# Turning five of the seven blocks of an FFT stage by DMA transposes: a long-convolution layer's backward pass on one Trainium2 core

## The chip, the cores and the metric

The program runs on one core of a Trainium2 chip. The metric is device time in microseconds (us), the median of several runs. One further execution was recorded by the hardware profiler; times inside the kernel are counted from the start of that execution's span.

## What is computed

The reference runs a small network forward and returns its output and the gradients of eight inputs. Two layers A (a gated long convolution) and B (a dense block) alternate, each around a layer norm and a residual; both A layers share their weights, and so do both B layers.

```python
def A(q, k, v, shift_k, ssm_k, ssm_D):        # B=1, S=2048, D=448
    k_shift = sum(shifted(k, t) * shift_k[:, 3 - t] for t in range(4))
    kv = k_shift * v
    y = irfft(rfft(pad(kv)) * rfft(pad(ssm_k)))[:S]   # FFT of length 4096
    return q * (y + kv * ssm_D)

def B(x, w1, w2):                             # F=1792
    return silu(x @ w1) @ w2

x = A_q
x = x + A(layernorm(x), ...);  x = x + B(layernorm(x), w1, w2)
x = x + A(layernorm(x), ...);  x = x + B(layernorm(x), w1, w2)
# outputs: x, and d(x . grad_out) / d(A_q, A_k, A_v, shift_k, ssm_k, ssm_D, w1, w2)
```

All tensors are bf16. The convolution's own gradient needs the spectrum of the output gradient, its products with the saved spectra of `kv` and of `ssm_k`, and two inverse transforms.

## The kernel before

The work is in three parts.

**Prefix** (`_ssm_prefix`): the spectra of `ssm_k` and `kv`, the convolution's output, and stores of the spectra to DRAM. Here two blocks of an FFT stage are already turned by DMA transposes (L426), the other five on TensorE.

**Main** (`Main.run`): forward and backward of the layers over four chunks of 512 rows. The dense layers' operands for the weight gradients are turned by DMA transposes on SP's queue (`store`, L595: one of 128x2048 elements, 512 KB, and one of 128x1536, 384 KB, per half) and written to DRAM (`put`, L601).

**Suffix** (`_ssm_suffix`): the convolution's backward pass. The output gradient's FFT has two stages. The first (`_s1_gy`, L218) is a set of matmuls whose results are copied into `A1g`, a tile of 128 partitions by 14336 elements, seen as 7 blocks of 16 squares of 128x128. Every square must be turned before the second stage. In the loop `for g in range(7)` at L1177, `_turn64` (L225) does that on TensorE: 32 transposes of half a row block each into PSUM, and one copy of 128x2048 (`_copy`, L116 on ACT or L117 on DVE, chosen by a running balance `bal`) into the block `Z[g]` of the tile `B1v`. Then `spectrum(cp)` runs the second stage for block `cp` (L236) and writes it back over `Z[cp]` (L1191), and `inverse(cp, ...)` multiplies by the saved spectra and runs the first inverse stage (L265). Its results go to `B1k`, which lies over the memory of `A1g`, and to `B1v`. So `A1g` may be overwritten only once all blocks have been turned out of it.

**Jobs.** TensorE's order is the program's (`manual_schedule`). Wherever the suffix would leave TensorE waiting it calls `jobs.run(n)`, which issues n groups of four matmuls of the weight gradients (`mms`, L1038, tile `ps_d`). Every output tile of a weight gradient takes two sets of 16 such matmuls; each set reads one stationary tile `dstat` of 128x2048 elements, 512 KB, that `load` (L1030) brings from DRAM on SP's queue. There are four slots for `dstat`, used in turn, so a load waits until the set that read its slot four loads earlier has been issued and done:

```python
st = self.stat[:, self.n_st % 4]
self.last_ld = nc.sync.dma_start(out=st, in_=src[:, ft, :, :])
```

SP's queue is worked off in the order of the program: an instruction that waits there holds back all that follow. At the change, the order on this queue in the program of before is: four `dstat` loads, the last at 516.56 us, then the load at 521.32, the load at 527.07, the load at 531.44, the load of `n3m` (L1099, 1792 KB), and further `dstat` loads. The saved spectra (`spec_load`, L1172 and L1173) come on POOL's queue.

Of the kernel before, what the change touches and what calls it, by code (L numbers as in the profile page):

```python
# [11 lines left out]
BF16 = mybir.dt.bfloat16  # L12
# [5 lines left out]
P = 128  # L18
# [95 lines left out]
def _copy(nc, eng, out, in_):  # L114
    if eng is nc.scalar:
        return nc.scalar.copy(out, in_)  # L116
    return eng.tensor_copy(out, in_)  # L117
# [18 lines left out]
def kernel(  # L136
# [63 lines left out]
    with tc.manual_schedule(engines={nc.tensor.engine}):  # L200
        with ExitStack() as es:
            Main(k, es).run(ys)
        _ssm_suffix(k)
# [18 lines left out]
def _turn64(k, pt, i, src):  # L222
    for r in range(2):
        rs = slice(64 * r, 64 * r + 64)
        k.nc.tensor.transpose(pt[:, r, i, :], src[rs], k.ident[rs, rs])  # L225
# [912 lines left out]
def _ssm_suffix(k):  # L1138
    nc, tc, bal = k.nc, k.tc, k.bal
# [3 lines left out]
    psum = k.psum  # L1143
    mm = dict(tag="mm", bufs=2)
    k.pt = dict(s1=mm, s2=mm, v=mm)
    A1 = k.A1g
    with ExitStack() as es:
# [12 lines left out]
        Z = [B1v_[:, 16 * g:16 * g + 16, :] for g in range(7)]  # L1160
# [3 lines left out]
        A1f = A1[:].rearrange("p a c n s -> p (a c n s)").rearrange("p (a b) -> p a b", b=P)  # L1164

        def spec_load(cp):
            lo, hi = cp * 2048, (cp + 1) * 2048
            if cp % 2:
                kk = [kk1[:, i] for i in range(2)]
            else:  # L1170
                kk = [sp.tile([P, 2048], BF16, name="kk_d", tag="gK", bufs=2)[:] for i in range(2)]
            nc.gpsimd.dma_start(out=kk[0], in_=k.SPEC_d["K"][:, lo:hi])  # L1172
            k.last_sp = nc.gpsimd.dma_start(out=kk[1], in_=k.SPEC_d["KV"][:, lo:hi])  # L1173
            return kk

        kks = [spec_load(0)]
        for g in range(7):  # L1177
            pt = psum.tile([P, 2, 16, 64], BF16, name="ps_tr", **mm)
            for i in range(16):
                _turn64(k, pt, i, A1f[:, 16 * g + i, :])  # L1180
            _copy(nc, bal.pick(2048, dve_ns=0.53), Z[g].rearrange("p i (r x) -> p r i x", r=2), pt[:])
            jobs.run(1)
        kks.append(spec_load(1))

# [182 lines left out]
```

## Time and profile before

| | |
|---|---|
| Median of 3 runs | 704.69 us (704.58 to 705.24) |
| The profiled execution's own time | 704.52 us |
| Its span, first to last instruction | 702.7 us |
| Granted TensorE clock, mean | 0.997 |
| PE (matmul) busy | 671.8 us, 96% |
| PE weight loads busy | 359.8 us, 51% |
| DVE / ACT / POOL busy | 484.3 / 432.2 / 101.0 us |
| Hardware DMA queue q1 (SP and ACT) | 111.78 MB, 58.3% of 16 engines' span |
| Software DMA queue q0 (POOL) | 36.29 MB, 15.2% |
| Instruction fetches, queue q8 | 46 packets, 0.75 MB |

The profiled execution takes 1.82 us more than its span, and 0.17 us less than the median of the runs. A busy PE says little by itself, since matmuls overlap; the chain of waits and the timeline of a stage say what the stage waits for. A DMA's row gives the time in which its queue's engine issued it, and apart from that the time from issue to landing. Losses on SP's queue do not show as idle time of SP.

### The profile page before, as it was taken

Reading aid. Unit: us, or ns where it says so; the run is one execution under the profiler, and the core shown is the slowest. Engines: PE = TensorE matmul, PEld = TensorE weight load, DVE = VectorE, ACT = ScalarE, POOL = GpSimd, SP = SyncE. Lnnn points to the kernel's source line nnn. Section 1 sums busy time; section 2 is a strip of 40 time slices with the busy share of each in tenths; the row PEclk is TensorE's granted clock in tenths of the full one; section 3 lists DMA queues with packets and bytes.
Section 4 is the critical chain, followed back from the end, with each engine's and each line's share of the span. In section 5 each row is a group of like instructions: output and inputs, shape, how many; then the busy total and the mean of one; then the engine's idle time right before and its main releaser. Section 6 shows DMA issues by size and latency. Waiting matters only on the chain.

```text
span 702.7 us, 14555 instructions
## 1 busy us (share of the span) xinstructions
PE 671.8 (96%) x5897; PEld 359.8 (51%) x5933; DVE 484.3 (69%) x1131; ACT 432.2 (62%) x522; POOL 101.0 (14%) x173
## 2 busy tenths in 40 slices
PE   6998789999999999999999999999999999999996
PEld 5876555454444444444444334444555555555664
DVE  5689862676889948889568884753946555538991
ACT  4988766968866957669577585223655453554431
POOL 1047110110011100111100100010111211102311
PEclk9999999999999999999999999999999999999999
DMA  8999948459898987487676599959567888966981
GB/s 315 260 272 304 351 137 212 112 109 260 217 225 240 245 195 184 137 236 202 203 180 180 159 227 335 288 168 218 187 225 268 309 273 317 349 190 215 330 292 42
DMA packets 199797, 161.03 MB, mean 229 GB/s; under 512 B 147697, under 2 KB 180212, under 8 KB 198962
## 3 DMA queue, kind: packets, MB, share of 16 engines
q1 hardware_dynamic: 184550, 111.78, 58.3%
q0 software_dynamic: 10368, 36.29, 15.2%
q10 hardware_dynamic: 4812, 12.04, 5.2%
q8 instruction: 46, 0.75, 0.4%
q14 instruction: 21, 0.17, 0.1%
HBM read 66.05 MB, written 54.60 MB: 172 GB/s over the span
## 4 chain that ended last, share of the span: by engine, by line
PE 59%; DVE 19%; issue 10%; ACT 5%; DMA 3%; POOL 3%; ACTq 0%; POOLq 0%; DVEq 0%
PE ps_d L1038 18%; PE ps_n L828 9%; PE ps_h L638 7%; PE ps_g L638 6%; PE ps_o L790 5%; DMA w2sb<-in_B_w_dram 3%; DVE ln_st L301 2%; PE ps_v L265 2%; PE ps_cv L449 2%; POOL rstd L306 2%; DVE lb_v L986 2%; PE ps_h L642 2%; DVE n L309 1%; DVE X L794 1%; PE ps_g L642 1%
## 5 line engine op out<-in xcount | busy, mean ns | idle before, releaser
L1038 PEld LDWEIGHTS <-dstat 128*128 128x128 bf16 x896 | 84.0, 98 | 77.8 <-issue 4.0
L828 PE MATMUL ps_n<-w1T,ghT 128*128 128x448 bf16 x448 | 97.0, 353 | 1.6 <-DVE ghT L813 1.3
L790 PE MATMUL ps_o<-w2sb,aT 128*128 128x448 bf16 x448 | 89.3, 353 | 0.2
L638 PE MATMUL ps_h<-nT,w1sb 128*128 128x512 bf16 (+1 forms) x408 | 84.2, 336 | 3.5 <-ACT Dall L116 2.2
L116 ACT CAST ghT<-ps_g 128x1024 bf16<-128x1024 f32 (+1 forms) x54 | 47.8, 900 | 59.4 <-PE ps_g L642 40.2
L638 PE MATMUL ps_g<-nT,w2T 128*128 128x512 bf16 x319 | 78.0, 380 | 2.1 <-DVE Dall L117 0.5
L828 PEld LDWEIGHTS <-ghT 128*128 128x128 bf16 x448 | 40.7, 98 | 50.5 <-issue 8.0
L790 PEld LDWEIGHTS <-aT 128*128 128x128 bf16 x448 | 43.0, 98 | 40.7 <-issue 2.6
L638 PEld LDWEIGHTS <-w1sb 128*128 128x128 bf16 x420 | 39.2, 98 | 39.0 <-issue 9.8
L773 ACT ACTIVATE aT<-ps_h 128x1024 bf16<-128x1024 f32 (+1 forms) x48 | 44.2, 920 | 20.4 <-PE ps_h L642 12.7
L986 DVE SCALAR_TENSOR_TENSOR lb_v<-lb_u,n 128x448 bf16<-128x448 bf16 x60 | 37.2, 619 | 25.4 <-ACT lb_u L832 24.9
L116 ACT CAST Dall<-ps_h 128x1024 bf16<-128x1024 f32 (+2 forms) x60 | 54.3, 906 | 0.0
L783 ACT ACTIVATE Dall<-Dall 128x1024 bf16<-128x1024 bf16 (+1 forms) x48 | 53.2, 1186 | 0.1
L638 PEld LDWEIGHTS <-w2T 128*128 128x128 bf16 x336 | 31.3, 98 | 41.9 <-issue 7.1
L306 POOL TENSOR_TENSOR rstd<-ln_ve,mhalf 128x2 f32<-128x2 f32 (+1 forms) x24 | 19.6, 818 | 220.7 <-DVE ln_ve L305 220.7
L1038 PE MATMUL ps_d<-X,dstat 128*128 128x448 bf16 x224 | 47.9, 353 | 0.0
L1038 PE MATMUL ps_d<-go,dstat 128*128 128x448 bf16 x224 | 47.2, 353 | 0.0
L1038 PE MATMUL ps_d<-n3m,dstat 128*128 128x448 bf16 x224 | 46.4, 353 | 0.0
L1038 PE MATMUL ps_d<-n1m,dstat 128*128 128x448 bf16 x224 | 46.3, 353 | 0.0
L832 ACT ACTIVATE lb_u<-ps_n,rstd 128x448 bf16<-128x448 f32 x32 | 20.6, 644 | 29.1 <-PE ps_n L828 21.2
L116 ACT CAST A1g<-ps_v 128x1024 bf16<-128x1024 f32 x14 | 14.9, 1065 | 36.5 <-PE ps_v L265 36.5
L794 DVE TENSOR_TENSOR X<-X,ps_o 128x448 bf16<-128x448 bf16 x32 | 19.5, 611 | 21.7 <-PE ps_o L790 21.7
(206 smaller groups left out, 1120.2 us busy)
## 6 DMA issues: line engine op xcount, KB each, us to landing
dstat<-a_d SPq DMA_DIRECT2D x28, 512.0 KB, 4.9
dstat<-g_d SPq DMA_DIRECT2D x28, 512.0 KB, 5.4
a_d<-turned SPq DMA_DIRECT2D x16, 512.0 KB, 3.0
g_d<-turned SPq DMA_DIRECT2D x16, 512.0 KB, 3.0
a_d<-turned SPq DMA_DIRECT2D x16, 384.0 KB, 2.7
g_d<-turned SPq DMA_DIRECT2D x16, 384.0 KB, 3.1
spec_K<-KAB POOLq DMA_DIRECT2D x7, 512.0 KB, 5.7
KAB<-KAB POOLq DMA_DIRECT2D x28, 128.0 KB, 5.0
```

The lines of the kernel that those rows point to most:

```text
L116: return nc.scalar.copy(out, in_)
L306: nc.gpsimd.tensor_tensor(out=r[:, lo:hi], in0=ve[:, lo:hi], in1=k.mhalf[:, lo:hi], op=ALU.pow)
L638: self.nc.tensor.matmul(ps, lhsT=w[:, b, ft * P:(ft + 1) * P], rhs=x[:, b], start=(start and b == 0), stop=(stop and b == bs[2]))
L642: self.nc.tensor.matmul(ps, lhsT=w[sl, b, ft * P:(ft + 1) * P], rhs=x[sl, b], start=start, stop=stop)
L773: self.last_silu = nc.scalar.activation(aT[hh][:, o:o + hi - lo, :], ps[:, lo:hi, :], ACT.Silu)
L783: self.nc.scalar.activation(dT[hh][:, o:o + n, :], dT[hh][:, o:o + n, :], ACT.Derivative_silu)
L790: nc.tensor.matmul(po[:, :D], lhsT=aT[ft // 7][:, ft % 7, tl * P:(tl + 1) * P], rhs=self.w2sb[:, ft, :], start=(ft == 0), stop=(ft == NF - 1))
L794: self.last_o = nc.vector.tensor_tensor(out=X[:, t, :], in0=X[:, t, :], in1=po[:, :D], op=ALU.add)
L828: nc.tensor.matmul(pn[:, :D], lhsT=gh[ft // 7][:, ft % 7, tl * P:(tl + 1) * P], rhs=self.w1T[:, ft, :], start=(ft == 0), stop=(ft == NF - 1))
L832: nc.scalar.activation(u0[:], pn[:, :D], ACT.Identity, scale=k.rstd[2 * L + 1][:, t:t + 1], accum_out=cp[:, tl, 0:1])
L986: nc.vector.scalar_tensor_tensor(out=v[:], in0=u0, scalar=-1.0 / D, in1=n_t, op0=ALU.mult, op1=ALU.mult, accum_out=cp[:, 1:2])
L1038: self.nc.tensor.matmul(ps[:, :D], lhsT=st[:, t, :], rhs=mov[:, t, :], start=(first and t == 0), stop=(last and t == NT - 1))
```

## The change

For blocks 2 to 6 the turn on TensorE with its copy is left out. In its place five DMA transposes of 128x2048 elements are put on SP's queue ahead of the loop, each from a block of `A1g` to the same `Z[g]`. Blocks 0 and 1 are turned as before, and the loop's seven `jobs.run(1)` stay.

```diff
         kks = [spec_load(0)]
+        for g in range(2, 7):
+            nc.sync.dma_start_transpose(out=Z[g], in_=A1f[:, 16 * g:16 * g + 16, :].rearrange("p a b -> p (a b)"))
         for g in range(7):
-            pt = psum.tile([P, 2, 16, 64], BF16, name="ps_tr", **mm)
-            for i in range(16):
-                _turn64(k, pt, i, A1f[:, 16 * g + i, :])
-            _copy(nc, bal.pick(2048, dve_ns=0.53), Z[g].rearrange("p i (r x) -> p r i x", r=2), pt[:])
+            if g < 2:
+                pt = psum.tile([P, 2, 16, 64], BF16, name="ps_tr", **mm)
+                for i in range(16):
+                    _turn64(k, pt, i, A1f[:, 16 * g + i, :])
+                _copy(nc, bal.pick(2048, dve_ns=0.53), Z[g].rearrange("p i (r x) -> p r i x", r=2), pt[:])
             jobs.run(1)
         kks.append(spec_load(1))
```

In the built program the five transposes stand on SP's queue between the `dstat` load that went at 516.56 us in the profile of before and the one that went at 521.32. The first of them waits for the copies into `A1g`. The order of all other instructions on PE, DVE, ACT and POOL is that of before, without the five turns and their copies (three on DVE, two on ACT). The first copy into `B1k` (ACT, L116, `A1g<-ps_v`) waits in addition for all five transposes.

## The prediction

> **What bounds the kernel now.** I read the page's chain that ended last first.
>
> ```profile
> PE 59%; DVE 19%; issue 10%; ACT 5%; DMA 3%; POOL 3%; ACTq 0%; POOLq 0%; DVEq 0%
> ```
>
> PE carries it. In order of time the chain lies on PE without a break from 511 to 632 us (ps_d and ps_v alone), then on DVE, and PE's busy time still fills the span to 690. So what the suffix's first half gains or loses on PE moves the end by as much, unless DVE's stretch from 637 to 685 were pinned by something else; it starts when PE's ps_gkv results arrive (DVE sat idle 7.77 us for the first at 633.34), so it moves along.
>
> Next the timeline of the stage, which shows what a turn costs:
>
> ```profile
> 516.99 0.93 ACT L116 CAST A1g<-ps_s 128x896 bf16<-128x896 f32 x1
> ...
> 518.35 0.52 PEld L225 LDWEIGHTS <-A1g 64*128 64x128 bf16 x32 [0.37 <-ACT A1g L116]
> ...
> 519.78 0.52 PEld L225 LDWEIGHTS <-A1g 64*128 64x128 bf16 x32 [0.37 <-issue]
> ...
> 521.80 0.93 PE L1038 MATMUL ps_d<-X,dstat 128*128 128x448 bf16 x4
> ...
> 534.93 3.19 PE L1038 MATMUL ps_d<-go,dstat 128*128 128x448 bf16 x16
> ...
> 537.96 2.43 PE L1038 MATMUL ps_d<-X,dstat 128*128 128x448 bf16 x12
> ```
>
> A1g is complete at 516.99 + 0.93 = 517.92. Turns start 1.43 us apart, with four ps_d matmuls in each step.
>
> Last, SP's queue, the lines of its loads and transposes one at a time. First the dstat loads at 516.56 (call it load A) and 521.32 (load B), then the transposes of L595 at 450.0, 481.2 and 475.2 with the landing line of each, then L426's two.
>
> ```profile
> 516.56 0.32 SPq L1030 DMA_DIRECT2D dstat<-a_d  x1
> 521.32 0.32 SPq L1030 DMA_DIRECT2D dstat<-a_d  x1
> ...
> L595 SPq DMA_TRANSPOSE turned<-ghT x1: 1610/1610/1610, 450.0 to 450.0; - x1
> DMA to landing us min/median/max: 3.8/3.8/3.8
> ...
> L595 SPq DMA_TRANSPOSE turned<-ghT x1: 1557/1557/1557, 481.2 to 481.2; - x1
> DMA to landing us min/median/max: 3.9/3.9/3.9
> ...
> L595 SPq DMA_TRANSPOSE turned<-ghT x1: 1783/1783/1783, 475.2 to 475.2; - x1
> DMA to landing us min/median/max: 5.4/5.4/5.4
> ...
> L426 SPq DMA_TRANSPOSE KAB<-KAB x2: 3879/4429/4979, 21.7 to 26.8; - x2
> DMA to landing us min/median/max: 7.6/8.0/8.4
> ```
>
> L426's two have the shape and the kind (SBUF to SBUF) of the new five; L595's larger half has it too. Issue takes 1.4 to 6.1 us, landing 3.3 to 8.4.
>
> **The change, part by part.**
>
> *Removed from PE.* Sixteen ps_d matmuls take 537.96 - 534.93 = 3.03 us, so four take 0.76. A turn thus costs 1.43 - 0.76 = 0.67 us, its 0.37 us of idle weight loading included. Five give 3.4 us. The copies (three of 1.22 us on DVE, two of 1.86 on ACT) cost nothing before and bring nothing: both engines then wait for PE (DVE 4.18 us before its next product). All PE work from 521.2 on could come 3.4 us earlier.
>
> *Added to SP.* Five transposes stand between load A and load B. The first can start when A1g is complete, at about 518.0. All dstat loads from B on, and n3m, are queued behind them. B's slot is free at 521.3, so before it left at 521.32; now it leaves when the fifth transpose has been issued, and its data come after theirs.
>
> *Who waits for that.* With four slots, load B is read by the fourth set after the one that ended at 521.3: X from 521.80, go from 527.55, X from 531.25, and go from 534.93. Load B is thus due at 534.93 before, and at 534.93 - 3.4 = 531.5 after. The cover of B is 531.5 - 521.3 = 10.2 us, against a landing of 3.4 to 8.2 us in this stage. Load A is due at 531.25 - 3.4 = 527.8 and lands 6.7 us after 516.56, at 523.3: safe.
>
> *When the transposes are through.* Pace: the two that follow each other from 450.0 move 896 KB, at 282 to 292 GB/s in nearly every slice of that window, in about 3.5 us: 2.0 us per 512 KB. Start: with nothing ahead, the first lands 3.8 us after issue, 521.8. With load A ahead it is later: the transpose at 418.7, behind a dstat load and a store, landed after 7.1 us, and those of L426 stood behind the input loads. Load A shares its engines with POOL's spectra until 521 and lands at 523.3; I take the first transpose to be through one pace later, 525.3. That is 7.3 us after issue, near the 7.1 row. Then four more at 2.0: 533.3.
>
> *Load B.* The dstat load issued at 482.82, right behind the transpose of 481.16, landed 4.0 us later, at 486.8; the transpose itself landed at 481.16 + 3.9 = 485.1. So a load lands 1.7 us after the transpose ahead of it. Load B lands at 533.3 + 1.7 = 535.0 and PE stands still for 535.0 - 531.5 = 3.5 us. The next load follows by one pace of a load (512 KB at the 400 GB/s of this stage's full slices, 1.3 us) and is due 3.03 us later; n3m is used only with the first g_d loads (from 568). No second stall in this sum.
>
> *Sum.* 704.52 - 3.4 + 3.5 = 704.6, which is 704.8 on the scale of the median (0.17 above the profiled run). With a first transpose a little less held back by load A (half a microsecond) it is 704.3. I take 704.6.
>
> *Bounds of the unknown term.* Best: load A does not hold the first transpose; the last lands at 521.8 + 4 x 2.0 = 529.8, B at 531.5, no stall. Worst: the pace of L426, 4.43 us of SP's time each; B leaves at 518.0 + 22.1 = 540.1 and lands 3.4 us later, 543.5: a stall of 12.0.
>
> *Edits that cost nothing.* Z[2] is read first by the second stage at 547.91 before, 544.5 after; even the worst case has it by 530. The copy into B1k that now waits for all five transposes is due at 541.02 - 3.4 = 537.6, 4.3 us after my last landing; beyond that it would hold ACT, but B's stall moves it along. A1g's memory is not touched earlier.
>
> *A rule for the speed of a transpose.* The trace's rate is 282 to 292 GB/s while one runs alone. [...]
>
> **The rivals.**
>
> *Faster, 701.3 to 703.2: the transposes run beside load A.* The queue has 16 engines, and transposes could start on those that are done with A. Stall 0 to 2.0 us, time 704.69 - 3.4 + 0 to 2.0. For it: L595's median landing is 4.1 us, though many of its transposes follow other traffic. Against: the 7.1 to 8.4 us rows above.
>
> *Slower, 706.1 to 709.3: one held-up engine holds up the whole transpose.* The transpose at 475.2 lasted 5.4 us to landing, not 3.8:
>
> ```profile
> GB/s 421 393 418 430 440 461 346 237 144 106 293 288 258 242 398 270 270 266 51 9 0 0 0 2 7 10 9 10 9 65 292 292 287 278 16 0 0 0 0 0
> ...
> q8 instruction: 1, 0.02, 1.5%
> ```
>
> In this window (475 to 481 us, 0.15 us a slice) the rate falls to 0 for 1.5 us in the middle of the transpose, and one instruction fetch lies in it. In 518 to 531 us before there were two such fetches. They are 16 KB, and there are 46 for PE's 11,830 instructions, one per 257; without 320 of them I expect only the one near load A's end, already in my start. A second fetch, or POOL's 112 KB stores at the wrong moment, adds about 1.6 us each. It decides from a last landing of 534.7, a pace of 2.35 us in place of 2.0. At 3.1 (the pair at 485.6 needed 3.50 us to issue and 6.4 to land) the last lands at 525.3 + 12.4 = 537.7, B at 539.4: stall 7.9, 709.2. At L426's pace it is 704.69 - 3.4 + 12.0 = 713.3.
>
> [...]
>
> *No effect: the turns are not on the path.* If DVE's stretch after 637 had slack to give, a shift of PE would not reach the end and the time stays 704.7. Against: DVE's idle 7.77 us for PE.
>
> **How the numbers follow.** Forecast (stall 2.0 to 4.8): 0.40. Beside load A: 0.25. Held-up engines: 0.32. No effect: 0.03. 0.2% is 1.4 us, about what a measurement of this kernel can tell from no change. Faster 0.25, same 0.40 + 0.03 = 0.43, slower 0.32. The forecast's own range is 703.3 to 706.1. The whole range leaves out the best end, under 701.9 (stall under 0.6), and the slow tail beyond a pace of 3.1, each about one in ten: 701.9 to 709.2.
>
> **What would show it.** In the profile after: no L225 at 521 to 527 and ps_d back to back there; five transposes on SP from 518.0, issue times of 1.5 to 3.5 us, landings about 2 us apart, the last near 533; the next dstat load leaving after 526 in place of 521.32; PE idle 2 to 5 us ahead of a ps_d<-go set at about 531.5, released by DMA. No such idle time means the faster rival; gaps in the transposes' rate beside instruction fetches, and a longer stall, mean the slower one. I am wrong in kind if PE's loss lies elsewhere, at the copy into B1k or at Z[2].

## The result, and the profile after

| | before | after |
|---|---|---|
| Median | 704.38 us (703.32 to 705.24, 6 runs) | 709.67 us (708.05 to 710.15, 6 runs) |
| Ratio to before, 95% interval | | 1.0068 (1.0057 to 1.0078) |
| The profiled execution | 704.52 us, span 702.7 | 708.84 us, span 707.1 |
| Granted TensorE clock, mean | 0.997 | 0.993 |

The changed kernel is slower, by 5.3 us between the medians. The forecast was 704.6 (no change that can be measured), and the median lies 0.5 us above the upper end of its range. In the profiled execution of after the whole stage runs 1.02 us earlier than in that of before (`A1g` complete at 516.9 in place of 517.9), so times of before are lowered by 1.02 where the two are compared.

The page first: the chain that ended last, and the group of L1038 that works on `go`. After the bar stand busy time, mean ns of one, and the idle time ahead of the group with what ended most of it.

```profile
PE 56%; DVE 18%; issue 10%; ACT 5%; DMA 4%; POOL 3%; SPq 2%; ACTq 0%; POOLq 0%; DVEq 0%
...
L1038 PE MATMUL ps_d<-go,dstat 128*128 128x448 bf16 x224 | 48.5, 360 | 7.1 <-DMA dstat<-a_d 7.1
```

SP's queue, which was not on the chain before, holds 2% of it, and these matmuls of the weight gradients wait 7.1 us for a load. The same group on the page of before:

```profile
L1038 PE MATMUL ps_d<-go,dstat 128*128 128x448 bf16 x224 | 47.2, 353 | 0.0
```

It had no idle time then, and its busy time was 47.2 us in place of 48.5: the work itself became longer too, by 1.3 us.

The line of the transposes (issue times, then landing), and the timeline of SP around it:

```profile
L1178 SPq DMA_TRANSPOSE B1v<-A1g x5: 2060/2650/5017, 517.0 to 530.1; - x5
...
DMA to landing us min/median/max: 4.6/4.8/8.4
```

```profile
516.98 15.77 SPq L1178 DMA_TRANSPOSE B1v<-A1g  x5
532.86 1.67 SPq L1030 DMA_DIRECT2D dstat<-a_d  x3
```

The first transpose landed 8.4 us after its issue, at 525.4; the last, 4.8 after 530.1, at 534.9. Load B left at 532.86; before, it had left at 521.32, which is 520.30 lowered. The timeline of PE:

```profile
529.75 0.93 PE L1038 MATMUL ps_d<-X,dstat 128*128 128x448 bf16 x4
537.83 4.52 PE L1038 MATMUL ps_d<-go,dstat 128*128 128x448 bf16 x16 [7.15 <-DMA dstat<-a_d]
```

PE is ready at 530.68 and stands until 537.83. Then the set takes 4.52 us, where the same sixteen took 3.19 before. The table by stretches shows why (busy time and count of PE, PEld, DVE, ACT, POOL; then the granted clock, the DMA share and GB/s):

```profile
530.00:533.00 3.00, 0.68 (x4) 0.14 (x2) 2.95 (x5) 2.27 (x3) 0.44 (x1) 1.00 1.13 207
533.00:536.00 3.00, 0.00 (x0) 0.00 (x0) 2.93 (x5) 0.00 (x0) 0.10 (x1) 0.62 1.07 220
536.00:537.70 1.70, 0.00 (x0) 0.00 (x0) 0.72 (x2) 0.00 (x0) 0.54 (x1) 0.50 0.96 357
537.70:540.50 2.80, 2.67 (x8) 1.12 (x9) 0.00 (x0) 0.00 (x0) 0.00 (x0) 0.50 1.06 422
540.50:543.00 2.50, 2.50 (x15) 1.30 (x14) 0.00 (x0) 0.00 (x0) 0.00 (x0) 0.99 1.00 424
```

While PE stands, its granted clock falls from 1.00 to 0.50, and it stays there until about 540.5, some 2.7 us into the set. (A later run, in which PE works through this time at 1.00, shows that the standing brings the fall about.) The mean of 0.62 from 533 to 536 puts the fall at about 533.7, 3.0 us after the last matmul. In the run of the transposes alone, below, the clock was full again only after 5.6 us of work.

Taken together: with the turns gone the set could start 3.4 us earlier, at 534.93 - 1.02 - 3.4 = 530.5; it starts 7.3 us after that (the 7.15 in the line count only from the end of the matmul ahead), and it takes 1.33 us longer. That is 5.2 us more.

### The profile page after: what moved, and what is told of

It is laid out like the page before. It is cut to its first block, busy times and chain, and to the rows that moved or that the text cites. A ratio compares the mean times of both kernels' runs of the same rounds, so it can differ in the third digit from the quotient of the medians.

```text
span 707.1 us, 14247 instructions
## 1 busy us (share of the span) xinstructions
PE 666.6 (94%) x5737; PEld 355.6 (50%) x5773; DVE 480.6 (68%) x1128; ACT 428.5 (61%) x520; POOL 101.1 (14%) x173
## 4 chain that ended last, share of the span: by engine, by line
PE 56%; DVE 18%; issue 10%; ACT 5%; DMA 4%; POOL 3%; SPq 2%; ACTq 0%; POOLq 0%; DVEq 0%
PE ps_d L1038 17%; PE ps_n L828 9%; PE ps_h L638 7%; PE ps_g L638 6%; PE ps_o L790 5%; DMA w2sb<-in_B_w_dram 2%; DVE ln_st L301 2%; SPq L1178 2%; PE ps_v L265 2%; PE ps_cv L449 2%; POOL rstd L306 2%; DVE lb_v L986 2%; PE ps_h L642 2%; DVE n L309 1%; DVE X L794 1%
## 5 line engine op out<-in xcount | busy, mean ns | idle before, releaser
L1038 PEld LDWEIGHTS <-dstat 128*128 128x128 bf16 x896 | 84.7, 98 | 86.8 <-DMA dstat<-a_d 7.6
L116 ACT CAST ghT<-ps_g 128x1024 bf16<-128x1024 f32 (+1 forms) x54 | 47.8, 900 | 59.4 <-PE ps_g L642 40.2
L1038 PE MATMUL ps_d<-go,dstat 128*128 128x448 bf16 x224 | 48.5, 360 | 7.1 <-DMA dstat<-a_d 7.1
L116 ACT CAST Dall<-ps_h 128x1024 bf16<-128x1024 f32 (+2 forms) x60 | 54.3, 904 | 0.0
L1038 PE MATMUL ps_d<-X,dstat 128*128 128x448 bf16 x224 | 47.4, 353 | 0.0
L1038 PE MATMUL ps_d<-n3m,dstat 128*128 128x448 bf16 x224 | 46.4, 353 | 0.0
L1038 PE MATMUL ps_d<-n1m,dstat 128*128 128x448 bf16 x224 | 46.3, 353 | 0.0
L116 ACT CAST A1g<-ps_v 128x1024 bf16<-128x1024 f32 x14 | 15.0, 1070 | 45.1 <-PE ps_v L265 32.1
```

Source lines behind the costliest of these rows:

```text
L1038: self.nc.tensor.matmul(ps[:, :D], lhsT=st[:, t, :], rhs=mov[:, t, :], start=(first and t == 0), stop=(last and t == NT - 1))
```

## The experiments

The theory after this profile: the five turns are worth what was estimated; what is lost is the load that stands behind the transposes on SP's queue, with the clock that falls while PE waits for it. Against it stood: the turns were worth less; the transposes do harm by themselves, in any order; the slow set has another cause.

### The turns alone

```diff
-            nc.sync.dma_start_transpose(out=Z[g], in_=A1f[:, 16 * g:16 * g + 16, :].rearrange("p a b -> p (a b)"))
+            nc.gpsimd.memset(Z[g], 0.0)
```

> Blocks 2 to 6 are not turned at all; POOL, idle there, fills them with zeros, so that part of the computation is left out. This prices the removal alone. If the five turns are on the path: 704.4 - 3.4 = 701.0 us, and the dstat loads leave as before. Rival, the turns are not on the path and the loss of the changed kernel is something else: 704.4 us.

Measured: 700.58 us (699.98 to 701.3) against 704.67 for before, ratio 0.9947 (0.993 to 0.9963). That is 2.6 to 4.9 us less, with 3.4 in it. PE waits for nothing between 516 and 550 us here, and the set that reads load B runs at its old length:

```profile
517.54 0.64 PE L225 MATMUL ps_tr<-ident,A1g 64*128 64x64 bf16 x32
...
530.72 3.19 PE L1038 MATMUL ps_d<-go,dstat 128*128 128x448 bf16 x16
```

From the first turn to this set are 530.72 - 517.54 = 13.18 us; before, they were 534.93 - 518.35 = 16.58, so the trace too has 3.4. So the gain is there to be had, and PE's shift in this stage reaches the end of the kernel.

### The transposes alone

Before, with all seven turns, and five transposes of the same blocks into free memory at the same place of SP's queue.

```diff
...
+        for g in range(2, 7):
+            nc.sync.dma_start_transpose(out=scr[g - 2], in_=A1f[:, 16 * g:16 * g + 16, :].rearrange("p a b -> p (a b)"))
...
```

> The kernel before with all seven turns on TensorE, plus the five DMA transposes at the same place of SP's queue into memory that is free then. This prices the addition alone. Queue theory (the dstat loads stand behind the transposes on SP's queue): load B lands some 4.9 us after the fifth transpose has been issued, 16 us later than before, against a cover of 13.6 us, so PE stands about 3.8 us and may lose up to 1.4 us more to a lower clock after the stand: 708.2 to 709.6 us. Rival (the loss comes from the removal, for instance a changed order of copies, or from late blocks Z): about 704.4 us.

Measured: 710.48 us (708.72 to 712.29), ratio 1.0084 (1.0055 to 1.0114). The timeline of PE shows the same place:

```profile
539.88 5.99 PE L1038 MATMUL ps_d<-go,dstat 128*128 128x448 bf16 x16 [3.76 <-DMA dstat<-a_d]
```

The granted clock, behind the busy times as above, ahead of the set, during it and behind it:

```profile
536.20:538.70 2.50, 0.00 (x0) 0.00 (x0) 2.44 (x5) 1.50 (x3) 0.54 (x1) 1.00 1.06 241
538.80:545.50 6.70, 5.62 (x16) 2.29 (x17) 3.32 (x5) 0.00 (x0) 0.54 (x1) 0.50 1.02 394
545.60:548.00 2.40, 2.40 (x14) 1.08 (x12) 0.00 (x0) 0.00 (x0) 0.00 (x0) 1.00 0.92 383
```

3.76 us of waiting and 5.99 - 3.19 = 2.80 of slow clock, 6.6 us; this profiled execution, 712.29, is the longest of the four. The median is 0.9 us above the upper end of what the theory expected, which had put the clock at 1.4 us at most. It is nearly the time of after, although five turns more are done: the wait is shorter by about what the turns take (3.76 against 7.15). Once load B is late, its landing and the slow clock behind it set the time, and what PE saves ahead of it only lengthens the wait.

The shorter wait has the larger loss by the clock. The clock was at half for about 6.8 us in both runs, from 538.7 to 545.5 here and from 533.7 to 540.5 in after, but PE worked for 5.6 us of that time here and for 2.7 in after. Half of the time worked at half clock is lost: 2.8 and 1.35 us, against 2.80 and 1.33 measured.

### The loads on another queue

After, with load B and the two behind it issued by POOL in place of SP.

```diff
+POOL_LD = (16, 17, 18)
...
-            self.last_ld = nc.sync.dma_start(out=st, in_=src[:, ft, :, :])
+            self.last_ld = (nc.gpsimd if i in POOL_LD else nc.sync).dma_start(out=st, in_=src[:, ft, :, :])
```

> The changed kernel with the three dstat loads that stood behind the transposes on POOL's queue; all else, the five transposes too, unchanged. Queue theory: they leave when their slots are free (the first near 520.4 us), share the DMA engines with the transposes and land in time: 701 to 703 us, no wait of PE for dstat. Rival (the transposes fill the 16 DMA engines, whatever queue a load is on): the first load lands no earlier than about 535 us, PE stands over 4 us and the time stays above 706 us.

Measured: 716.46 us (708.88 to 717.22), ratio 1.0145 (1.0089 to 1.02). Three of the four executions took 716.4 to 717.2 us, one 708.88; the trace is of one of the three, and what the other did differently stays open. Neither expectation fits: the wait for load B is gone, which speaks against the rival, but the transposes suffer. PE's timeline, the line of the transposes, then ACT's timeline:

```profile
531.57 3.19 PE L1041 MATMUL ps_d<-go,dstat 128*128 128x448 bf16 x16
...
540.35 3.20 PE L1041 MATMUL ps_d<-go,dstat 128*128 128x448 bf16 x16 [1.41 <-DMA dstat<-a_d]
550.69 1.95 PE L265 MATMUL ps_v<-Gsb,pab 64*128 64x64 bf16 x64 [7.14 <-ACT A1g L116]
556.14 3.17 PE L1041 MATMUL ps_d<-X,dstat 128*128 128x448 bf16 x8 [3.50 <-DMA dstat<-a_d]
```

```profile
L1181 SPq DMA_TRANSPOSE B1v<-A1g x5: 4373/5534/7043, 518.0 to 540.0; - x5
...
DMA to landing us min/median/max: 9.5/10.1/13.3
```

```profile
549.62 1.02 ACT L116 CAST A1g<-ps_v 128x1024 bf16<-128x1024 f32 x1 [16.30 <-DMA B1v<-A1g]
```

Three loads of 512 KB on the other queue stretch the five issues from 15.8 to 29.0 us. The loss moves to the copy into `B1k`, which waits for the last transpose, and PE waits 7.1 us for that copy. It also waits 1.41 us for the third load on POOL's queue and 3.50 for the next one, which left SP's queue only behind the transposes, from 547.8 on. So there are two bounds: the loads must not stand behind the transposes, and the transposes must be through before that copy.

### The order on SP's queue, first try

After, with the order: load A, two transposes, load B, one transpose, the next load (C), two transposes, the next load (D), `n3m`.

```diff
-        for g in range(2, 7):
...
+        def turn_dma(*gs):
...
+        turn_dma(2, 3)
...
+            if cp == 0:
+                with tc.issue_after(jobs.last_ld.ins):
+                    turn_dma(4)
...
+                if ci == 0:
+                    with tc.issue_after(jobs.last_ld.ins):
+                        turn_dma(5, 6)
```

> The changed kernel with the transposes put between the loads on SP's queue: two, load, one, load, two, load. Queue theory: the first two loads land in time (near 529 and 533 us against 530.5 and 533.5), the last transpose near 537 us, just when its source is to be overwritten; what is left is at most 2 us of waits there or for the load behind n3m: 701 to 703.5 us. Rival (engines full): the loads share the same 16 engines and PE stands as long as in the changed kernel in several smaller pieces: 706 us or more.

Measured: 709.95 us (709.02 to 710.82), ratio 1.0076 (1.0051 to 1.0102). No better than after, but the wait has moved, as PE's timeline shows:

```profile
532.30 3.19 PE L1038 MATMUL ps_d<-go,dstat 128*128 128x448 bf16 x16
...
542.84 4.48 PE L1038 MATMUL ps_d<-go,dstat 128*128 128x448 bf16 x16 [2.91 <-DMA dstat<-a_d]
551.22 2.15 PE L1038 MATMUL ps_d<-X,dstat 128*128 128x448 bf16 x8 [2.86 <-DMA dstat<-a_d]
```

Load B is in time; load D, behind the last two transposes, is not, and neither is the load behind `n3m`, for which PE waits a second time. The clock fell here too (the set took 4.48 us in place of 3.19). The theory had at most 2 us of waits; there are 5.8, and the time is what its rival, full engines, asked for. Whether the order or the engines cost it is decided by the second try, below.

### Two blocks and three blocks

After, with fewer blocks turned by DMA (`range(5, 7)` and `g < 5`; `range(4, 7)` and `g < 4`):

```diff
-        for g in range(2, 7):
+        for g in range(5, 7):
...
-            if g < 2:
+            if g < 5:
```

> Only blocks 5 and 6 are turned by DMA transposes; blocks 0 to 4 stay on TensorE. Theory (the transposes are cheap, and the loss is the load that stands behind them): two turns less give 2 x 0.67 = 1.3 us; with the first transpose landed 8.4 us after its issue at 517 to 518, at about 526, and the second 2.4 later, load B lands 2.8 behind that, at about 531, against a due time of 534.93 - 1.3 = 533.6 in the time of before. No stall, no clock loss: 704.4 - 1.3 = 703.1, a ratio of 0.998. Rival (transposes beside the stage's other transfers cost something by themselves, whatever the order of the queue): 704.4 or more, a ratio of 1.000 or above, without a wait of PE for dstat.

> Blocks 4, 5 and 6 are turned by DMA transposes, blocks 0 to 3 on TensorE. Theory (the loss is the load behind the last transpose): three turns less give 2.0 us; the third transpose lands at about 526 + 2 x 2.4 = 530.8, load B 2.8 later at 533.6, due at 534.93 - 2.0 = 532.9. A wait of 0 to 1 us, too short for the clock to fall: 702.4 to 703.4, a ratio of 0.997 to 0.9985, the minimum of the curve over the number of blocks (none 704.4, two 703.1, three 702.9, five 709.7). Rival (each transpose costs by itself): the curve rises from none on, so more than the time with two blocks and more than 704.4.

Measured: 703.07 us (701.57 to 704.27) with two, ratio 0.997 (0.9953 to 0.9988); 702.85 (701.66 to 705.3) with three, ratio 0.9979 (0.9957 to 1.0001), both against 704.86 for before. Two blocks are faster; three are between faster and the same, and the two can't be told apart. PE's timeline, with two blocks and then with three:

```profile
533.48 3.19 PE L1038 MATMUL ps_d<-go,dstat 128*128 128x448 bf16 x16
```

```profile
533.02 3.20 PE L1038 MATMUL ps_d<-go,dstat 128*128 128x448 bf16 x16 [0.47 <-DMA dstat<-a_d]
```

With two there is no wait; with three it is 0.47 us, and the clock holds (3.20 us). Both medians lie where the theory had them. Up to here a transpose costs nothing that can be measured; the cost begins when the load behind it becomes late.

### The clock

After, with 37 matmuls of the same form put where PE stood still. Their results are overwritten by the set that follows.

```diff
+                if keys[0] == ("a", 1) and ft == 8:
+                    for _ in range(37):
+                        self.nc.tensor.matmul(ps[ft][:, :D], lhsT=self.k.ident[:], rhs=self.go[:, 0, :], start=True, stop=True)
```

> The changed kernel, and ahead of the set that reads load B 37 matmuls of 128x448 whose results that set overwrites (no operand of them comes by DMA at this time): about 7 us of work in the place where PE stood still. Theory (PE's clock fell because it stood still): the set takes 3.2 us in place of 4.5 and its granted clock is near 1.0; the time is 1.3 us less than the changed kernel's, 708.3, a ratio of 1.0055 to the kernel before. The wait for load B itself stays, now hidden in the added work. Rival (the set is slow for another cause, such as the transfers that run at that time or the late following matmuls): the set still takes 4.5 us, 709.7, a ratio of 1.0075.

Measured: 708.76 us (707.14 to 710.36), ratio 1.0053 (1.0035 to 1.0071). PE's timeline, and then the stretch of the set with the granted clock behind the busy times:

```profile
531.29 7.16 PE L1059 MATMUL ps_d<-go,ident 128*128 128x448 bf16 x37
538.29 3.19 PE L1038 MATMUL ps_d<-go,dstat 128*128 128x448 bf16 x16
```

```profile
538.00:541.50 3.50, 3.50 (x20) 1.69 (x19) 0.00 (x0) 0.00 (x0) 0.36 (x1) 1.00 1.08 439
```

The set takes 3.19 us again, at full clock, with the same wait for the load hidden in work that nobody needs. So the set of after was slow because PE had stood still. The set is 1.33 us shorter than in after; the time is about 1 us less by the medians, but the two intervals overlap, so only the trace settles the size.

### The order on SP's queue, second try

All five blocks by DMA; load B goes ahead of them into a buffer that is free (a fifth, beside the four slots), the later loads between them, `n3m` one block later. `ahead` issues a load early and keeps it for the set that reads it.

```diff
...
+        jobs.ahead(("a", 1), 8, True)
+        with tc.issue_after(jobs.last_ld.ins):
+            turn_dma(2, 3)
...
+                if ci == 0:
+                    with tc.issue_after(jobs.last_ld.ins):
+                        turn_dma(4)
+                        jobs.ahead(("a", 1), 9)
+                    with tc.issue_after(jobs.last_ld.ins):
+                        turn_dma(5, 6)
...
-            if cp == 0:
+            if cp == 1:
```

> All five blocks by DMA transposes, with the loads that the sets of this stage need put ahead and between: load B goes before the transposes into a buffer that is free by then, two transposes, the next load, and so on, and n3m goes one block later. Theory (only the order of the queue costs): no wait of PE for dstat of over 1 us in the stage, the gain of the five turns comes through but for the copy into B1k, which waits for the last transpose and has about 4 us of cover: 701.0 to 702.5, a ratio of 0.995 to 0.9975. Rival (the sixteen engines cannot carry five transposes, the loads and the traffic of the other queue in this time, in any order): a wait of some us remains somewhere, for a load or for the last transpose, and the time is 706 or more, a ratio above 1.002.

Measured: 702.19 us (699.93 to 703.36), ratio 0.996 (0.9943 to 0.9977): faster than both kernels. SP's timeline with the landing of the last two transposes, then PE's and ACT's timelines:

```profile
517.48 7.95 SPq L1185 DMA_TRANSPOSE B1v<-A1g  x2
525.54 0.52 SPq L1036 DMA_DIRECT2D dstat<-a_d  x1
526.10 3.71 SPq L1185 DMA_TRANSPOSE B1v<-A1g  x1
529.93 0.51 SPq L1036 DMA_DIRECT2D dstat<-a_d  x1
530.48 6.46 SPq L1185 DMA_TRANSPOSE B1v<-A1g  x2
537.04 4.71 SPq L1036 DMA_DIRECT2D dstat<-a_d  x4
...
L1185 SPq DMA_TRANSPOSE B1v<-A1g x2: 2893/3208/3522, 530.5 to 534.0; - x2
DMA to landing us min/median/max: 6.1/6.1/6.1
```

```profile
531.01 3.19 PE L1044 MATMUL ps_d<-go,dstat 128*128 128x448 bf16 x16
538.21 3.19 PE L1044 MATMUL ps_d<-go,dstat 128*128 128x448 bf16 x16
542.24 0.64 PE L265 MATMUL ps_v<-Gsb,pab 64*128 64x64 bf16 x32 [0.26 <-ACT B1v L116]
```

```profile
540.25 1.04 ACT L116 CAST A1g<-ps_v 128x1024 bf16<-128x1024 f32 x1 [7.48 <-issue]
```

Load B left ahead of the first of these lines. No set waits for `dstat`. The last transpose, issued at 534.0, landed 6.1 us later, at 540.1, and the copy into `B1k` ran right then; PE lost 0.26 us by it. The second bound is just met. The result can't be told from the kernel without the five turns (0.9947, 0.993 to 0.9963), so most of the 3.4 us comes through: the five transposes, the loads and POOL's traffic fit into this time, in this order and with the fifth buffer.

### One transpose in place of five

What was left open by these runs was the slow pace of the later transposes. After, with one instruction:

```diff
-        for g in range(2, 7):
-            nc.sync.dma_start_transpose(out=Z[g], in_=A1f[:, 16 * g:16 * g + 16, :].rearrange("p a b -> p (a b)"))
+        nc.sync.dma_start_transpose(out=B1v_[:, 32:112, :], in_=A1f[:, 32:112, :].rearrange("p a b -> p (a b)"))
```

> The changed kernel, with the five blocks turned by one DMA transpose of 128x10240 elements in place of five of 128x2048; place on the queue and bytes are the same. In the changed kernel the rate of the transposes was 285 to 295 GB/s for the first 3.7 us without a pause and 199 to 227 after that, and it fell in the same way in the other runs in their third block or later, while the one transpose of w1 (1.6 MB, from DRAM) held 283 to 295 to its end. Theory (the fall belongs to the succession of separate instructions): one instruction keeps 290, the last block lands at 525.4 + 4 x 1.81 = 532.6 in place of 534.9, load B 2.3 earlier, and the time is 2.3 us less than the changed kernel's: 707.4, a ratio of 1.0043. Rival (it belongs to the length of the stream, or to transposes from SBUF to SBUF): the rate falls to about 215 as before, and the time is that of the changed kernel, 709.7, a ratio of 1.0075.

Measured: 708.33 us (707.39 to 710.28), ratio 1.0054 (1.0038 to 1.0071). The rate in slices of 0.125 us, from 528 to 533 in after, and from 527 to 532 here:

```profile
GB/s 227 215 217 221 217 217 219 193 113 45 90 203 223 215 201 211 213 209 219 217 215 217 223 217 215 213 213 188 162 148 115 207 248 223 215 199 236 219 205 221
```

```profile
GB/s 287 291 291 291 289 289 291 291 291 291 321 272 294 706 18 350 98 281 283 293 293 287 291 293 293 283 293 293 287 291 291 295 283 293 289 291 291 291 291 287
```

(The slices around 528.6 hold a store of POOL's.) The fall to some 215 GB/s belongs to the succession of instructions, not to the length of the stream or to the direction. It need not wait for the third. In the second try, from 522 to 526 in slices of 0.1 us, it begins at 525.1, when the first of two transposes had just landed (at 517.5 + 7.4 = 524.9):

```profile
GB/s 38 13 18 0 0 0 3 8 8 10 8 10 10 10 64 279 294 287 297 287 289 289 252 294 292 287 294 287 297 287 284 279 261 246 238 228 225 220 212 220
```

In the run with two blocks the second went as fast as the first, at 285 to 295 GB/s. Why a later instruction in a row goes slower, and why not always the same one, stays open.

The time follows only in part. The transpose landed 16.9 us after its issue, where the five had taken 17.9. Load A landed 7.6 us after its issue here and 6.6 in after (from 5.2 to 7.8 over the traces of these kernels), and the data of the transposes started as it landed, at 523.0 in place of 522.0, which ate about half of what the pace gave. PE's timeline has

```profile
536.75 5.17 PE L1038 MATMUL ps_d<-go,dstat 128*128 128x448 bf16 x16 [5.92 <-DMA dstat<-a_d]
```

The wait is 1.2 us shorter than in after, and the set behind it, 5.17 us, is 0.65 longer: the clock was at half from about 534.0 to 540.8, again for 6.8 us, and PE worked for 4.0 of them. By the medians that is about 1 us less than after, inside the overlap of the intervals.

## Why the prediction was wrong

Right were the step that priced the turns (3.4 us; the kernel without them is 2.6 to 4.9 us faster, and 3.4 by its trace), the place of the loss (load B behind the transposes, PE waiting ahead of the set that reads it), and the claims that `Z[2]` and the copy into `B1k` cost nothing in this kernel and that no second stall follows.

Wrong was the sum at load B: three of its terms were too small, and the slow clock had no term at all. The forecast made the stall 3.5 us, so that it ate the gain exactly; counted as the forecast did, from the time at which the set was due, it is 537.8 - 530.5 = 7.3. All times of the forecast are lowered by 1.02 here.

- *First transpose through*, put at load A's landing plus one pace, 7.3 us after issue: it took 8.4, and came at 525.4 in place of 524.3. **1.1 us.** An instruction fetch lies in it. The forecast counted this fetch as part of its start, without a price of its own. In the window from 521.5 to 524 (slices of 0.0625 us):

```profile
GB/s 0 12 86 16 25 37 33 41 180 508 274 258 287 262 283 266 270 61 20 16 4 0 0 0 0 0 8 8 4 8 12 8 8 8 12 8 12 8 8 12
...
q8 instruction: 1, 0.02, 2.7%
```

  The transposes started at 522.0, as load A landed (515.5 + 6.6 = 522.1), and from 522.6 on moved almost nothing for 1.4 us. Without this gap the first would have been through ahead of the forecast's 524.3. A fetch of 16 KB stands just ahead of the gap, between 522.0 and 522.25. In the run with one transpose the fetch lies 1.3 us after the start of the data, between 524.25 and 524.5, and there the same gap runs from 524.8 to 526.2: it went with the fetch, not with a place in the transpose. That the one makes the other was not tried, since no run moved a fetch alone.
- *Four more at 2.0 us each*: 2.4 (9.5 us for four). **1.5 us.** The row behind the 2.0 was a pair of transposes, most of it at 282 to 294 GB/s and a quarter of its slices at 197 to 279. Here the first two go at 290, and from the third on it is 215. The last experiment shows this as the price of five instructions.
- *Load B 1.7 us behind the last transpose*: 2.9 in after, 2.7 in the run with one transpose. **1.2 us.** The row behind 1.7 was a load behind one transpose. Here further loads and `n3m` were issued within 2.3 us behind load B; whether they slowed it was not tried, and the cause of this term stays open.
- *No term for the clock*: **1.3 us** in after (4.52 against 3.19), 2.8 in the run that does both. The forecast priced a wait at its length. The run with 37 matmuls shows the term by itself.

The first three make the stall 3.8 us longer, 7.3 in place of 3.5; the fourth comes on top. With the 3.4 us of the turns that is 5.2 us more by the trace, against 5.3 by the medians.

Of the rivals, the slower one came nearest, though the median lies 0.4 us above its range too. A gap beside a single fetch, as it described one, is there in the first transpose, which came 1.1 us late; that the fetch makes the gap was not shown. Its condition, a pace above 2.35 us, was met (2.4), but for another reason than it gave. The faster rival fell: the first transpose began to move data only as load A landed (522.0 and 522.1). The best rate of an undisturbed stretch of transposes in any of these runs was 285 to 295 GB/s.

## What to carry to other kernels

The transposes put on SP's queue cost first of all what stood behind them there (load B left at 532.86 in place of 520.30). So for a DMA put on a queue list the loads that it delays, with their due times, and put those loads ahead of it before counting any gain. As long as the load behind was in time, the transposes cost nothing that could be measured here (two blocks, ratio 0.997, or five in the right order, 0.996); once it was late, its landing set the time, and everything saved ahead of it became waiting. A wait of TensorE costs more than its length when its clock falls: in the stage of these runs waits of 2.86 us and more brought it down, and waits of 1.41 and less did not. A wait of 2.45 us in the prefix (L253, for DVE) brought it down in before and, at the same place and as long, did not in after. The set of sixteen matmuls behind a wait for load B or D took 1.3 to 2.8 us longer, and not the more the longer the wait was.

## What the runs showed of the hardware that was not expected

- Back-to-back transposes of 512 KB went at 285 to 295 GB/s for the first one or two of a series and, in most series, at some 200 to 230 after that; one instruction for the same bytes went at 280 to 300 to its end, but for a gap of 1.4 us and a store of POOL's.
- Three loads of 512 KB on POOL's queue, beside the transposes of SP's, took their median issue from 2.65 to 5.53 us. Their 1.57 MB would need 3.9 us at the 400 GB/s of this stage's full slices; the five issues together lost 13.2.
- Once fallen, TensorE's granted clock stayed at 0.50 for 6.8 us in three runs (after, the transposes alone, one transpose) and for 3.4 in the first try of the order (542.1 to 545.5) and in the prefix of before (84.6 to 88.0), whether PE worked or stood. In the stage of these runs the fall came 2.1 (first try of the order) to 3.1 us (one transpose) after the last matmul. In the prefix of before it came 2.7 us after, when PE had been at work again for 0.2 us, and a second fall in the first try of the order came at 552.3, when PE had been at work again for 1.1 us (eight matmuls took 2.15 us there, against 1.69 in the second try).
